# Float64 weights joined by one VectorE instruction, their signs taken over by GpSimd, and maxima and splits over pairs of chunks

## The chip, the core and the metric

The kernel runs on one core of a Trainium2 chip. The metric is the device time of one execution in microseconds (us). The engines are named as in the profile: PE is TensorE's matmul and PEld its weight load, DVE is VectorE, ACT is ScalarE, POOL is GpSimd, SP is SyncE, which here issues all DMAs.

## The reference

Causal attention with a window of 128 and an ALiBi bias over 8 batches of 8 heads, 576 positions and 64 features, then a feed-forward layer over the 4608 tokens that come out. The sizes are 512 to 2048 to 512.

```python
scores = scale * np.matmul(q, k.transpose(0, 1, 3, 2))
scores = np.where(mask, scores + bias[None], -1000000000.0)
attn = np.exp(scores - np.max(scores, axis=-1, keepdims=True))
attn = attn / (np.sum(attn, axis=-1, keepdims=True) + 1e-09)
x = np.matmul(attn, v)                       # then to (4608, 512)
h = x @ w_in                                 # w_in  (512, 2048)
g = 0.5 * h * (1.0 + erf(h * inv_sqrt2))
return g @ w_out                             # w_out (2048, 512)
```

The weights arrive as float64: `np.random.randn(...)` times a factor, with no cast. The kernel must therefore make float32 values of 64-bit words on the chip, before it can use them.

## The kernel before, in words

**Stages.** Batch 0 of the attention runs in float32 (`softmax_first`, `turn`, `weigh`). Tile 0 of the feed-forward layer (512 tokens) follows: `mlp_in(0, ...)` on PE at L600, then `mlp_out(0, ...)`, half of it in float32 against the float32 weights `zo` (L654), half of it in float16 against `wo` (L661). Batch 1 of the attention runs between these matmuls. From then on there is one batch and one tile per turn, up to tile 8. Float16 operands are pairs of halves, high and low, scaled by a power of two.

**The weights.** They come in 16 chunks of 128 partitions by 1024 values, each value a pair of 32-bit words (`raw`): eight chunks of `w_in` (names `zi`, then `wi`) and eight of `w_out` (names `zo`, then `wo`). SP fetches them at L176 and L179. Each chunk goes through `to_float32` (L182):

- ACT, L190: the high word read as a float32, its absolute value times 2^-112 into `z`.
- ACT, L192: the low word turned into the three bits that follow the high word's mantissa, written over the low word as int32.
- DVE, L195: `z` limited from above, with its maximum as a by-product (`accum_out=stat`).
- DVE, L196: `z` shifted left by 3, joined with the low bits.
- DVE, L199: the sign bit of the high word joined in.

**Scales.** The maximum of each pair of chunks goes over the partitions with `partition_all_reduce` on POOL (L114). From it DVE makes a power of two, `pww`, and its inverse, `sww`. With these, `split_weights` (L203) makes the high half on ACT (L207) and the low half on DVE (L149), for each chunk by itself. For `w_out` there is one such scale for all eight chunks together, `stwo` (L259), from which `pwm`, `k2` and `s2` follow (L260 to L270). Without them no float16 `wo` can be made, and without `pwm` no output tile can be scaled.

**Other users of POOL at that time.** The same all-reduce serves the maxima of v for batches 0 and 1 (`stv`) and of q and k for batch 1 (`stq`); the q and k halves of batch 1, and so its scores, wait for `stq`. Memsets clear `kbuf`'s pad (L377), the rooms of `e_main` (L448, L449) and, as soon as DVE has written them, the masked corners of the scores (L442). From tile 1 on, POOL also scales `g` (L627), and from batch 3 on `e_main` (L519).

**The order.** Each engine works through its own queue in order. Which order that is, a scheduler decides when the program is built. Where an instruction of POOL needs a routine that is not in the library that GpSimd holds, the built program has an instruction ahead of it that reloads the library. The order prints that as `ISA` with no tile behind it. Library 1 holds the all-reduce, library 0 holds `tensor_scalar`; memsets need neither. The program has three such reloads: of library 0 near the start (it is resident then), of library 1 ahead of the first all-reduce, and of library 0 ahead of the first L627.

Of the kernel before, what the change touches and what calls it, by code (L numbers as in the profile page):

```python
# [20 lines left out]
P = 128  # L21
# [37 lines left out]
def attention_gelu_mlp(  # L59
# [14 lines left out]
    def small(shape, name, bufs, tag=None, dt=F32):  # L74
        return pool.tile(shape, dt, tag=tag or name, name=name, bufs=bufs)
# [34 lines left out]
    def over_partitions(stat, n, early=False, floor=FLOOR):  # L110


        if early:
            nc.gpsimd.partition_all_reduce(stat, stat, P, bass_isa.ReduceOp.max)  # L114
            nc.vector.tensor_scalar_max(stat, stat, floor)
# [44 lines left out]
    hi_thr = 122848.0 * SQUEEZE  # L160
    STAT_FLOOR = 2.0 ** ((127 - 50) // 8 - 127) * (1 + (127 - 50) % 8 / 8)
    assert FLOOR == 2.0 ** -50
    NW = NCC * 256

    raws = {}
# [13 lines left out]
            nc.sync.dma_start(flat.rearrange("p (c f) -> p c f", c=2), w_out_v[:, 2 * m : 2 * m + 2, :])  # L179
        raws[n] = raw  # L180

    def to_float32(n, z, stat):  # L182
# [12 lines left out]
        nc.vector.tensor_scalar(z, z, hi_thr, None, op0=ALU.min, op1=ALU.max, accum_out=stat)  # L195
        nc.vector.scalar_tensor_tensor(  # L196
            out=zi, in0=zi, scalar=3, in1=lo, op0=ALU.logical_shift_left, op1=ALU.bitwise_or
        )
        nc.vector.scalar_tensor_tensor(  # L199
            out=zi, in0=hi, scalar=-0x80000000, in1=zi, op0=ALU.bitwise_and, op1=ALU.bitwise_or  # L200
        )

    def split_weights(z, both, scale):  # L203

        hi = both[:, 0].rearrange("p c f -> p (c f)")
        lo = both[:, 1].rearrange("p c f -> p (c f)")
        nc.scalar.activation(hi, z, AF.Copy, scale=scale)  # L207
        low_part(lo, z, scale, hi)

    def pow2_of_words(dst, stat):  # L210

        nc.vector.tensor_scalar(
            dst.bitcast(I32), stat.bitcast(I32), 3, EXPMASK, op0=ALU.logical_shift_left, op1=ALU.bitwise_and
        )

    def absmax(dst, src, axis=AX.X):
        nc.vector.tensor_reduce(out=dst, in_=src, axis=axis, op=ALU.max, apply_absolute_value=True)  # L217
# [4 lines left out]
    pwo = pool.tile([P, NWP], F32, name="pwo")  # L222
    stwo = pool.tile([P, NWP], F32, name="stwo")

    def weights_in(ns, gate=None):

        zs = {}
        stat = small([P, len(ns)], f"stw{ns[0]}", 1)
        for n in ns:
            if n % 2 == 0:  # L230
                tag, bufs = Z_TAGS[n // 2]
                zz = pool.tile([P, 2, NW], F32, tag=tag, name=f"zi{n}", bufs=bufs)
            zs[n] = zz[:, n % 2]
            if gate is not None:
                nc.vector.tensor_copy(zs[n][:, 0:1], gate)
            to_float32(n, zs[n], stat[:, n - ns[0] : n - ns[0] + 1])
        over_partitions(stat, len(ns), True, STAT_FLOOR)
        r = slice(ns[0], ns[-1] + 1)

        nc.vector.tensor_tensor(out=stat[:, 0:1], in0=stat[:, 0:1], in1=stat[:, 1:2], op=ALU.max)  # L240
        pow2_of_words(pww[:, r], stat[:, 0:1].broadcast_to([P, len(ns)]))
        inverse(sww[:, r], pww[:, r], 12)
        tile_scales(0, ns)
        for n in ns:
            both = pool.tile([P, 2, NCC, 256], F16, name=f"wi{n}")
            split_weights(zs[n], both, sww[:, n : n + 1])
            wi.append(both)

    def weights_out_raw(m):

        if m % 2 == 0:
            zo.append(pool.tile([P, 2, NW], F32, tag="wo", name=f"zo{m}", bufs=4))
            zo.append(zo[m])
        to_float32(NWP + m, zo[m][:, m % 2], stwo[:, m : m + 1])

    def weights_out_scale():


        over_partitions(stwo, NWP, True, STAT_FLOOR)  # L259
        pow2_of_words(pwo, stwo)  # L260
        nc.vector.tensor_tensor(out=pwo, in0=pwo, in1=pww, op=ALU.mult)
# [13 lines left out]
    def weights_out_split(m):  # L275

        tag, bufs = ("wo", 4) if m else ("ld", 2)
        both = pool.tile([P, 2, 2, 2, DM], F16, tag=tag, name=f"wo{m}", bufs=bufs)
        for k in range(2):
            split_weights(zo[m + k][:, k], both[:, k], s2[:, m + k : m + k + 1])  # L280
            wo[m + k] = both[:, k]
        held.append(both)
        if m + 2 == NWP:
            first = pool.tile([P, 2, 2, 2, DM], F16, tag="wo", name="wo_first", bufs=4)
            nc.sync.dma_start(first, held[0])
            wo[0], wo[1] = first[:, 0], first[:, 1]
# [940 lines left out]
```

## Time and profile before

| what | us |
|---|---|
| median of 3 runs (lowest, highest) | 940.12 (938.73, 943.64) |
| span of the profiled execution, first to last instruction | 936.4 |
| busy in it: PE, DVE, ACT, POOL | 900.2, 737.2, 555.9, 199.0 |
| first `mlp_in` matmul on PE | 72.97 |
| all-reduce of `stq`, of `stwo` (start) | 106.07, 115.91 |

The span is 3.7 us below the median, for what lies around the first and the last instruction. In a timeline a row gives start, length, engine, line, operation, tiles and, in brackets, the engine's idle time ahead of it with what ended that. In a row by line or tile, the numbers behind the bar are busy us in total and the mean length of one in ns; three numbers with slashes are the least, the median and the greatest length in ns.

### The profile page before, as it was taken

Reading aid. Unit: us, or ns where it says so; the run is one execution under the profiler, and the core shown is the slowest. Engines: PE = TensorE matmul, PEld = TensorE weight load, DVE = VectorE, ACT = ScalarE, POOL = GpSimd, SP = SyncE. Lnnn points to the kernel's source line nnn. Section 1 sums busy time; section 2 is a strip of 40 time slices with the busy share of each in tenths; the row PEclk is TensorE's granted clock in tenths of the full one; section 3 lists DMA queues with packets and bytes.
Section 4 is the critical chain, followed back from the end, with each engine's and each line's share of the span. In section 5 each row is a group of like instructions: output and inputs, shape, how many; then the busy total and the mean of one; then the engine's idle time right before and its main releaser. Section 6 shows DMA issues by size and latency. Waiting matters only on the chain.

```text
span 936.4 us, 18792 instructions
## 1 busy us (share of the span) xinstructions
PE 900.2 (96%) x7500; PEld 487.0 (52%) x7500; DVE 737.2 (79%) x1445; ACT 555.9 (59%) x1175; POOL 199.0 (21%) x412
## 2 busy tenths in 40 slices
PE   7969999779999899999999999999999999999998
PEld 3544444434454445444454445444444444488887
DVE  6898989779876877678767877687646898999771
ACT  5977958777673566256435643575465545744760
POOL 1010000013201443135303531164114540000000
PEclk9989999999999999999999999999999999999999
DMA  9518433872456133614562446224402351001001
GB/s 319 215 46 298 173 107 74 199 203 57 86 137 157 36 66 78 197 36 76 97 164 69 62 102 176 69 51 83 104 13 51 71 84 46 1 12 35 1 1 46
DMA packets 173512, 91.26 MB, mean 97 GB/s; under 512 B 132592, under 2 KB 155248, under 8 KB 173296
## 3 DMA queue, kind: packets, MB, share of 16 engines
q1 hardware_dynamic: 173424, 90.06, 38.6%
q8 instruction: 59, 0.97, 0.4%
q14 instruction: 29, 0.24, 0.1%
HBM read 46.53 MB, written 9.44 MB: 60 GB/s over the span
## 4 chain that ended last, share of the span: by engine, by line
PE 53%; DVE 19%; ACT 8%; DMA 4%; issue 3%; SPq 1%; POOL 0%; POOLq 0%; DVEq 0%; ACTq 0%
PE o L661 22%; PE h L600 17%; PE av L559 3%; PE sc L415 3%; DMA v<-vp 2%; ACT s L510 2%; PE u L860 2%; PE u_out L947 2%; DVE g L149 2%; DVE e_main L149 2%; DVE nmax L507 1%; PE v L860 1%; DMA et<-e_main 1%; DVE stv L217 1%; DVE s L437 1%
## 5 line engine op out<-in xcount | busy, mean ns | idle before, releaser
L600 PE MATMUL h<-x,wi 128*128 128x512 f16 x1536 | 341.1, 380 | 6.1 <-ACT g L626 3.1
L600 PEld LDWEIGHTS <-wi 128*128 128x128 f16 x1536 | 147.5, 98 | 184.7 <-issue 9.0
L661 PE MATMUL o<-wo,g 128*128 128x512 f16 x936 | 213.0, 380 | 1.1 <-DVE wo L149 1.1
L661 PEld LDWEIGHTS <-g 128*128 128x128 f16 x1248 | 117.2, 98 | 141.5 <-issue 2.3
L510 ACT ACTIVATE s<-s,nmax 128x192 f32<-128x192 f32 x252 | 111.2, 442 | 96.9 <-DVE nmax L507 93.3
L627 POOL TENSOR_SCALAR g<-g,sg 128x512 f16<-128x512 f32 x96 | 77.9, 817 | 192.0 <-ACT g L626 189.8
L149 DVE SCALAR_TENSOR_TENSOR e_main<-s,z,e_main 128x192 f16<-128x192 f32 x252 | 107.0, 468 | 13.1 <-POOL e_main L519 8.9
L519 POOL TENSOR_SCALAR e_main<-s,z 128x192 f16<-128x192 f32 x180 | 93.0, 534 | 86.9 <-issue 31.3
L626 ACT ACTIVATE g<-h,gs 128x512 f32<-128x512 f32 x96 | 63.9, 687 | 74.5 <-PE h L600 51.8
L149 DVE SCALAR_TENSOR_TENSOR g<-g,sg,g 128x512 f16<-128x512 f32 (+1 forms) x112 | 90.3, 824 | 21.0 <-POOL g L627 19.4
L415 PE MATMUL sc<-kbuf,qbuf 64*64 64x192 f16 (+1 forms) x1656 | 74.8, 263 | 9.2 <-DMA kbuf<-kp 4.5
L437 DVE SCALAR_TENSOR_TENSOR s<-sc,cs,bias_h 128x384 f32<-128x384 f32 x112 | 63.8, 608 | 12.2 <-PE sc L415 12.0
L661 PE MATMUL o<-wo_first,g 128*128 128x512 f16 x312 | 71.8, 379 | 0.1
L507 DVE TENSOR_REDUCE nmax<-s 128x5 f32<-128x960 f32 (+1 forms) x56 | 58.6, 1046 | 2.2 <-POOL s L442 0.2
L442 POOL MEMSET s<- 64x128 f32 (+1 forms) x112 | 19.1, 171 | 186.7 <-DVE s L437 186.1
L572 ACT ACTIVATE x<-av,cx 128x448 f16<-128x448 f32 (+6 forms) x52 | 23.5, 474 | 58.0 <-PE av L559 57.9
L415 PEld LDWEIGHTS <-qbuf 64*64 64x64 f16 x1512 | 36.0, 106 | 38.4 <-issue 36.9
L559 PE MATMUL av<-et,vbuf 128*64 128x128 f16 (+1 forms) x1680 | 44.1, 211 | 6.4 <-DMA et<-e_main 6.3
L559 PEld LDWEIGHTS <-vbuf 128*64 128x64 f16 x1680 | 41.0, 111 | 16.6 <-issue 11.3
L510 ACT ACTIVATION_READ_ACCUMULATOR s<-s,nmax 128x1 f32 x252 | 47.1, 187 | 0.0
L510 ACT ACT_TABLE_LOAD x29 | 37.2, 1283 | 7.9 <-DVE square L120 7.4
L947 PEld LDWEIGHTS <-g 128*128 128x128 f16 x384 | 37.6, 98 | 4.6
(268 smaller groups left out, 1159.7 us busy)
## 6 DMA issues: line engine op xcount, KB each, us to landing
v<-vp SPq DMA_DIRECT2D x32, 320.0 KB, 5.5
out<-ob SPq DMA_DIRECT2D x34, 256.0 KB, 2.3
raw<-w_in SPq DMA_DIRECT2D x8, 1024.0 KB, 13.7
raw<-w_out SPq DMA_DIRECT2D x8, 1024.0 KB, 5.1
q<-qp SPq DMA_DIRECT2D x7, 1152.0 KB, 6.2
k<-kp SPq DMA_DIRECT2D x7, 1152.0 KB, 6.3
qbuf<-qp SPq DMA_DIRECT2D x4, 288.0 KB, 4.9
kbuf<-kp SPq DMA_DIRECT2D x4, 288.0 KB, 5.2
```

Of the source, the lines that this page charges most:

```text
L149: nc.vector.scalar_tensor_tensor(out=dst, in0=src, scalar=scale, in1=high, op0=ALU.mult, op1=ALU.subtract)
L415: nc.tensor.matmul(ps[bank][o, n, 0:W], a, m, start=(i == 0), stop=(i == len(terms) - 1 and b > 0), skip_group_check=True,)
L437: nc.vector.scalar_tensor_tensor(out=s[:, bank[0] : bank[0] + k, :], in0=ps[bank][:, 0:k, 0:W], scalar=cs, in1=bias.broadcast_to([P, k, W] ...
L507: nc.vector.tensor_reduce(out=nmax[:, r], in_=s[:, r], axis=AX.X, op=ALU.max, negate=True)
L510: nc.scalar.activation(s[:, i, :], s[:, i, :], AF.Exp, bias=nmax[:, i : i + 1], accum_out=z[:, i : i + 1])
L519: nc.gpsimd.tensor_scalar(e[:, i, 0, c], s[:, i], z[:, i : i + 1], 1.0, op0=ALU.mult, op1=ALU.mult)
L559: nc.tensor.matmul(av[r, (j - blocks[0]) * QB : (j - blocks[0] + len(js)) * QB], v32s[b][:, hp, kb, r] if b < EXACT else vbuf[:, vi, hp, k ...
L600: nc.tensor.matmul(ph, wi[n][:, a, cc, k * P : (k + 1) * P], x[:, cc, b, :], start=(i == 0), stop=(i == 3 * NCC - 1),)
L626: nc.scalar.activation(g32, ph, AF.Gelu, scale=gsc[t, n])
L627: nc.gpsimd.tensor_scalar(g[:, r, 0], g32, gsg[t, n], 1.0, op0=ALU.mult, op1=ALU.mult)
L661: nc.tensor.matmul(o, both[:, a, c], wo[n][:, b, k, :], start=(fc == first and i == 0), stop=(fc == last and i == 2),)
L947: nc.tensor.matmul(ps[name][:, tb], f(d, a)[:, k, tb * P : (tb + 1) * P], w(d, b, k), start=first, stop=True, skip_group_check=True,)
```

## The change

**Each chunk.** The limit from above (L195) goes, and with it the maximum as a by-product. The sign is made in place on POOL: the upper 16 bits of the high word, read as int16, become -32768 or 0 (`tensor_scalar` with `is_lt` and `mult`, one per chunk, on 1024 values that stand 8 bytes apart). ACT writes the low bits as int16 into the lower 16 bits of the same high word. So the high word now holds sign and low bits, and one DVE instruction (L197 in the new file) shifts `z` and joins that word in. It waits for ACT and for POOL.

**Each pair of chunks.** A maximum over 2048 values replaces the two by-products (`absmax`, L211), one all-reduce has one column in place of two, and one ACT and one DVE instruction over 2048 values split the pair (L203, L150). For `w_out`, `stwo` has four columns in place of eight.

```diff
         zi = z.bitcast(I32)
+        quarters = raw.rearrange("p f w -> p (f w)").bitcast(I16).rearrange("p (f q) -> p f q", q=4)
+        low_bits, sign = quarters[:, :, 2], quarters[:, :, 3]
         nc.scalar.activation(z, hi.bitcast(F32), AF.Abs, scale=SQUEEZE)
+        nc.gpsimd.tensor_scalar(sign, sign, 0.0, -32768.0, op0=ALU.is_lt, op1=ALU.mult)
         nc.scalar.activation(
-            lo, lo.bitcast(U32), AF.Copy, bias=-0.5 + 7.5 * 2.0 ** -18, scale=2.0 ** -29 * (1 - 2.0 ** -18)
-        )
-        nc.vector.tensor_scalar(z, z, hi_thr, None, op0=ALU.min, op1=ALU.max, accum_out=stat)
-        nc.vector.scalar_tensor_tensor(
-            out=zi, in0=zi, scalar=3, in1=lo, op0=ALU.logical_shift_left, op1=ALU.bitwise_or
+            low_bits, lo.bitcast(U32), AF.Copy, bias=-0.5 + 7.5 * 2.0 ** -18, scale=2.0 ** -29 * (1 - 2.0 ** -18)
         )
         nc.vector.scalar_tensor_tensor(
-            out=zi, in0=hi, scalar=-0x80000000, in1=zi, op0=ALU.bitwise_and, op1=ALU.bitwise_or
+            out=zi, in0=zi, scalar=3, in1=hi, op0=ALU.logical_shift_left, op1=ALU.bitwise_or
         )
...
-            to_float32(n, zs[n], stat[:, n - ns[0] : n - ns[0] + 1])
-        over_partitions(stat, len(ns), True, STAT_FLOOR)
+            to_float32(2 * n + k, z[:, k])
+        z = z.rearrange("p k f -> p (k f)")
+        absmax(stat, z)
+        over_partitions(stat, 1, True)
...
-        for n in ns:
-            both = pool.tile([P, 2, NCC, 256], F16, name=f"wi{n}")
-            split_weights(zs[n], both, sww[:, n : n + 1])
+        both = pool.tile([P, 2, 2, NCC, 256], F16, name=f"wi{n}")
+        hi, lo = (both[:, a].rearrange("p k c f -> p (k c f)") for a in range(2))
+        split_weights(z, hi, lo, sww[:, 2 * n : 2 * n + 1])
...
-        to_float32(NWP + m, zo[m][:, m % 2], stwo[:, m : m + 1])
+        to_float32(NWP + m, zo[m][:, m % 2])
+        if m % 2:
+            absmax(stwo[:, m // 2 : m // 2 + 1], zo[m].rearrange("p k f -> p (k f)"))
```

**The order on POOL.** Before, from the first all-reduce (`stv` of batch 0) to that of `stwo`. L114 is the all-reduce, `stw` the maxima of a pair of `w_in` chunks, L377, L448 and L449 are memsets:

```order
L114 ISA
L114 ISA stv_307<-stv_307 128x1 [waits DVE_49]
L114 ISA stw_659<-stw_659 128x2 [waits DVE_49]
L377 MEMSET kbuf 128x2x128 [waits DMAHW1_49,DMAHW4_49,PE_49,Pool_49]
L114 ISA stw_686<-stw_686 128x2 [waits DVE_49]
L448 MEMSET e_main 128x10x64 [waits PE_49,Pool_49]
L114 ISA stw_715<-stw_715 128x2 [waits DVE_49]
L449 MEMSET e_main 128x8x64 [waits PE_49,Pool_49]
L114 ISA stw_744<-stw_744 128x2 [waits DVE_49]
L114 ISA stq_1141<-stq_1141 128x2 [waits DVE_49,Activation_49]
L114 ISA stv_1126<-stv_1126 128x1 [waits DVE_49]
L114 ISA stwo<-stwo 128x8 [waits DVE_49]
```

One reload stands ahead of the first all-reduce, and none follows among these. Now, on POOL, from the first all-reduce to that of the second pair (L115 is the all-reduce, L193 the sign, L373 and L444 memsets):

```order
L115 ISA stv_307<-stv_307 128x1 [waits DVE_49]
L193 ISA
L193 TENSOR_SCALAR raw_119<-raw_119 128x1024 [waits DMAHW6_49,Activation_49]
L193 TENSOR_SCALAR raw_121<-raw_121 128x1024 [waits DMAHW7_49,Activation_49]
L373 MEMSET kbuf 128x2x128 [waits DMAHW1_49,DMAHW4_49,PE_49,Pool_49]
L193 TENSOR_SCALAR raw_123<-raw_123 128x1024 [waits DMAHW0_49,Activation_49]
L193 TENSOR_SCALAR raw_125<-raw_125 128x1024 [waits DMAHW1_49,Activation_49]
L115 ISA
L115 ISA stw_659<-stw_659 128x1 [waits DVE_49]
L193 ISA
L193 TENSOR_SCALAR raw_127<-raw_127 128x1024 [waits DMAHW2_49,Activation_49]
L193 TENSOR_SCALAR raw_129<-raw_129 128x1024 [waits DMAHW3_49,Activation_49]
```

Signs and all-reduces alternate, and at each turn a reload stands between them. Between the all-reduce of `stv` and that of `stq` (batch 1) there are now 12 reloads, 13 signs, 5 all-reduces and the 3 memsets; in the whole program there are 17 reloads in place of 3. The place on POOL where `stq` and `stwo` stand (L438 are the memsets on the scores of batch 1):

```order
L115 ISA stq_1117<-stq_1117 128x2 [waits Activation_49]
L193 ISA
L193 TENSOR_SCALAR raw_977<-raw_977 128x1024 [waits DMAHW1_49,DVE_49,Activation_49]
L193 TENSOR_SCALAR raw_934<-raw_934 128x1024 [waits DMAHW2_49,DVE_49,Activation_49]
L193 TENSOR_SCALAR raw_1019<-raw_1019 128x1024 [waits DMAHW3_49,DVE_49,Activation_49]
L438 MEMSET s_0_1156 64x128 [waits DVE_49] x2
L438 MEMSET s_0_1156 64x64 [waits DVE_49]
L115 ISA
L115 ISA stwo<-stwo 128x4 [waits DVE_49]
```

The all-reduce of `stwo` has moved behind three memsets on the scores of batch 1, which themselves exist only after `stq`; before, it stood ahead of all of them.

More of the change, by code (lines that the diff above doesn't have):

```diff
@@ L13 @@
 I32 = mybir.dt.int32
+I16 = mybir.dt.int16
 U32 = mybir.dt.uint32
@@ L159, in attention_gelu_mlp @@
     SQUEEZE = 2.0 ** -112
[L160 to L162 removed]
+    NPW = NWP // 2
     NW = NCC * 256
@@ L221, in attention_gelu_mlp, with weights_in @@
     sww = pool.tile([P, NWP], F32, name="sww")
[L222 to L228, printed above, removed]
[L229 to L247 removed]
+    pwo = pool.tile([P, NPW], F32, name="pwo")
+    stwo = pool.tile([P, NPW], F32, name="stwo")
+    def weights_in(n, gate=None):
+        stat = small([P, 1], f"stw{n}", 1)
+        tag, bufs = Z_TAGS[n]
+        z = pool.tile([P, 2, NW], F32, tag=tag, name=f"zi{n}", bufs=bufs)
+        for k in range(2):
+            if gate is not None:
+                nc.vector.tensor_copy(z[:, k, 0:1], gate)
+            to_float32(2 * n + k, z[:, k])
+        z = z.rearrange("p k f -> p (k f)")
+        absmax(stat, z)
+        over_partitions(stat, 1, True)
+        r = slice(2 * n, 2 * n + 2)
+        pow2_of_words(pww[:, r], stat.broadcast_to([P, 2]))
+        inverse(sww[:, r], pww[:, r], 12)
+        tile_scales(0, [2 * n, 2 * n + 1])
+        both = pool.tile([P, 2, 2, NCC, 256], F16, name=f"wi{n}")
+        hi, lo = (both[:, a].rearrange("p k c f -> p (k c f)") for a in range(2))
+        split_weights(z, hi, lo, sww[:, 2 * n : 2 * n + 1])
+        wi.extend(both[:, :, k] for k in range(2))
     def weights_out_raw(m):
@@ L253, in weights_out_raw @@
             zo.append(zo[m])
[L254 removed]
+        to_float32(NWP + m, zo[m][:, m % 2])
+        if m % 2:
+            absmax(stwo[:, m // 2 : m // 2 + 1], zo[m].rearrange("p k f -> p (k f)"))
     def weights_out_scale():
[L259 removed]
+        over_partitions(stwo, NPW, True)
         pow2_of_words(pwo, stwo)
[L261 removed]
+        nc.vector.tensor_tensor(out=pwo, in0=pwo, in1=pww[:, 0:NWP:2], op=ALU.mult)
         most = pool.tile([P, 1], F32, name="most")
@@ L278, in weights_out_split @@
         both = pool.tile([P, 2, 2, 2, DM], F16, tag=tag, name=f"wo{m}", bufs=bufs)
+        hi, lo = (both[:, a].rearrange("p k c f -> p (k c f)") for a in range(2))
+        split_weights(zo[m].rearrange("p k f -> p (k f)"), hi, lo, s2[:, m : m + 1])
         for k in range(2):
-            split_weights(zo[m + k][:, k], both[:, k], s2[:, m + k : m + k + 1])
-            wo[m + k] = both[:, k]
+            wo[m + k] = both[:, :, k]
         held.append(both)
@@ L1067, in attention_gelu_mlp @@
     gates = [None, (1, 'z', 8), (2, 'z', 8), (3, 'z', 8)]
-    for n in range(0, NWP, 2):
-        g = gates[n // 2]
-        weights_in([n, n + 1], g and getattr(unit(0, g[0]), g[1])[:, g[2] : g[2] + 1])
+    for n in range(NPW):
+        g = gates[n]
+        weights_in(n, g and getattr(unit(0, g[0]), g[1])[:, g[2] : g[2] + 1])
     fetch(2)
```

12 lines of the change are left out of this document (4 added, 8 removed).

## The prediction, before the result was known

> **What bounds the kernel now.** The page comes first: it tells the busy shares and the chain of work that ended last.
>
> ```profile
> span 936.4 us, 18792 instructions
> PE 900.2 (96%) x7500; PEld 487.0 (52%) x7500; DVE 737.2 (79%) x1445; ACT 555.9 (59%) x1175; POOL 199.0 (21%) x412
> PE 53%; DVE 19%; ACT 8%; DMA 4%; issue 3%; SPq 1%; POOL 0%; POOLq 0%; DVEq 0%; ACTq 0%
> ```
>
> PE is busy for 96% of the span, and POOL has no share in the chain. But the change touches only the stage in which the weights are made ready, so the busy times by windows of 25 us come next (PE, PEld, DVE, ACT, POOL; then granted clock, DMA share, GB/s).
>
> ```profile
> 0.00:25.00 25.00, 19.25 (x137) 9.58 (x137) 16.13 (x41) 15.31 (x40) 2.57 (x14) 1.00 0.97 323
> 25.00:50.00 25.00, 22.91 (x199) 14.13 (x197) 20.70 (x59) 24.57 (x68) 2.20 (x3) 0.93 0.48 177
> 50.00:75.00 25.00, 17.19 (x124) 11.84 (x125) 24.54 (x51) 15.68 (x26) 3.40 (x5) 0.80 0.29 95
> 75.00:100.00 25.00, 25.00 (x118) 11.29 (x117) 22.54 (x36) 23.58 (x39) 0.00 (x0) 1.00 0.76 263
> 100.00:125.00 25.00, 25.00 (x95) 11.37 (x94) 24.96 (x40) 24.35 (x33) 2.16 (x3) 1.00 0.33 126
> ```
>
> Here DVE and ACT are the busy engines beside PE, and POOL works 10.33 us in 125 (the sum of its column). PE has idle time only before 75 us: 5.75, 2.09 and 7.81 us, 15.65 in all. A DVE that is relieved can win no more than that; POOL has much room, if its work doesn't have to stand in a row with what others wait for. So the last view is POOL's timeline of the stage (start, length, and in brackets the idle time ahead).
>
> ```profile
> 1.59 0.29 POOL masks.py:199 TENSOR_SCALAR_AFFINE_SELECT adders<-adders 128x128 bf16<-128x128 bf16 x1 [0.29 <-POOL kbuf L301]
> ...
> 19.37 0.38 POOL L114 PARTITION_ALL_REDUCE stv<-stv  x1 [16.36 <-DVE z L478]
> 26.11 1.26 POOL L114 PARTITION_ALL_REDUCE stw<-stw  x1 [6.36 <-DMA raw<-w_in]
> 30.30 0.31 POOL L377 MEMSET kbuf<- 128x256 f16 x1 [2.92 <-PE sc L415]
> 49.38 1.26 POOL L114 PARTITION_ALL_REDUCE stw<-stw  x1 [18.77 <-DVE zi L195]
> 52.99 0.63 POOL L448 MEMSET e_main<- 128x640 f16 x1 [2.35 <-PE tp L496]
> 56.55 0.35 POOL L114 PARTITION_ALL_REDUCE stw<-stw  x1 [2.92 <-DVE pww L212]
> 56.77 0.59 POOL L449 MEMSET e_main<- 128x512 f16 x1
> 66.82 1.32 POOL L114 PARTITION_ALL_REDUCE stw<-stw  x1 [9.45 <-DVE zi L195]
> 106.07 0.35 POOL L114 PARTITION_ALL_REDUCE stq<-stq  x1 [37.94 <-ACT kbuf L363]
> 108.00 0.37 POOL L114 PARTITION_ALL_REDUCE stv<-stv  x1 [1.57 <-DVE stq L115]
> 115.91 1.44 POOL L114 PARTITION_ALL_REDUCE stwo<-stwo  x1 [7.54 <-DVE zo L195]
> ...
> 132.15 0.14 POOL L442 MEMSET s<- 64x64 f32 x1 [0.71 <-DVE s L437]
> ```
>
> Between 19.75 (19.37 + 0.38) and 106.07 POOL has 86.32 us for five all-reduces and three memsets; that is the room into which 12 reloads and 13 signs are now put.
>
> **What DVE, ACT and PE win.** By line and form, up to 190 us (busy us, mean ns):
>
> ```profile
> L149 DVE SCALAR_TENSOR_TENSOR wi<-zi,sww,wi 128x1024 f16<-128x1024 f32 x8 | 10.1, 1280 | 0.0
> ...
> L199 DVE SCALAR_TENSOR_TENSOR zi<-raw,zi 128x1024 int32<-128x1024 int32 x8 | 9.8, 1223 | 0.0
> L196 DVE SCALAR_TENSOR_TENSOR zi<-zi,raw 128x1024 int32<-128x1024 int32 x8 | 9.7, 1227 | 0.0
> ...
> L195 DVE TENSOR_SCALAR_CACHE_REDUCE zi<-zi 128x1024 f32<-128x1024 f32 x8 | 9.7, 1213 | 0.0
> ...
> L217 DVE TENSOR_REDUCE stv<-v 128x1 f32<-128x2560 f32 x3 | 8.5, 2817 | 3.4 <-DMA v<-vp 3.4
> ...
> L149 DVE SCALAR_TENSOR_TENSOR vbuf<-v,scv,vbuf 128x2560 f16<-128x2560 f32 x1 | 2.9, 2886 | 0.0
> ```
>
> And ACT's high halves in the same view:
>
> ```profile
> L207 ACT ACTIVATE wi<-zi,sww 128x1024 f16<-128x1024 f32 x8 | 8.8, 1151 | 2.0 <-DVE sww L144 2.0
> ...
> L372 ACT ACTIVATE kbuf<-k,scq 128x2304 f16<-128x2304 f32 x1 | 2.3, 2304 | 0.0
> ```
>
> - Conversion, 16 chunks: three instructions (1.21 + 1.23 + 1.22 = 3.66) become one join (1.23) and half of a maximum over 2048 (2817 ns / 2560 = 1.10 ns per value, 2.25 for the pair, 1.13 per chunk). That saves 1.30 each, 21 us of DVE.
> - Low halves, 8 pairs: two of 1.28 become one of 2048 at 2886 / 2560 ns each, 2.31. That saves 0.25 each, 2 us. ACT saves as much on the high halves (two of 1.15 become one of 2.05 at 1.00 ns per value); its low-bits writes stay 16 in number, and that 16-bit writes cost it the same is an assumption. No DMA is added or taken away.
>
> Most of these 23 us lie beside PE's full windows after 75 us and are worth nothing there. They would count ahead of 75 us, and only where no wait takes their place.
>
> **What POOL gets: the sign.** No row shows a compare, an int16 operand or a stride of 8 bytes on POOL. The nearest are its other `tensor_scalar` lines (least, median, greatest ns):
>
> ```profile
> L627 POOL TENSOR_SCALAR g<-g,sg x96: 684/772/1819, 204.8 to 735.1; 128x512 f16<-128x512 f32 x96
> L519 POOL TENSOR_SCALAR e_main<-s,z x180: 418/425/1819, 316.5 to 770.6; 128x192 f16<-128x192 f32 x180
> ```
>
> From the fastest of both, (684 - 418) / 320 = 0.83 ns per value: 0.42 + 832 × 0.83 = 1.11 us for 1024 values. By the slowest L627, 1819 / 512 = 3.55 ns per value: 3.64 us. I take the slow end, since all three of those features are strange to the fast rows, and a stride gains nothing. It could be beyond: twice is 7.3.
>
> **What POOL gets: the reload.** An idle row bounds it from below: the affine select at 1.59 came 0.29 us after the memset, with a reload of the library that was already there. From above there are the 16.36 us ahead of the first all-reduce, which DVE ended and not the reload, so it is no more than that. What a reload does is to read code from DRAM; the nearest rows are the reads of the raw weights in the same stretch (issue to landing):
>
> ```profile
> DMA to landing us min/median/max: 5.0/7.5/14.7
> ```
>
> I take the median, 7.5 us, with all of 0.3 to 16.4 kept as bounds. I assume that none of it runs ahead: the signs behind it and the all-reduce before it stand in one queue, and code in use can't be overwritten.
>
> The GPSIMD Engine Reference of the Trainium skill (§ 2.1, Instruction dispatch) has about 6 us for the first call to a freshly loaded kernel, with no instruction to be seen. By that price in place of 7.5 the sum below would be 977 us of span, about 981; no run shown here bears on it.
>
> **The sum.** Call a reload p and a sign s. The order puts all of this in one row on POOL, and in it nothing can pass. The all-reduce of `stq` then starts no sooner than
>
> 19.75 + 12p + 13s + 4.56 (the five all-reduces: 1.26, 1.26, 0.35, 1.32, 0.37) + 1.53 (memsets: 0.31, 0.63, 0.59) = 25.84 + 12p + 13s.
>
> With 7.5 and 3.64 that is 163.2, where it was 106.07. This takes it that POOL never waits in this row for a raw chunk. SP fetches those in order, each as soon as a join has freed its room, and before, they ran ahead of the chain:
>
> ```profile
> 62.28 0.37 SPq L179 DMA_DIRECT2D raw<-w_out  x1
> ...
> 90.94 0.37 SPq L352 DMA_DIRECT2D k<-kp  x1
> ```
>
> Five chunks of `w_out` have their signs in this row, and k of batch 1, from which `stq` is made, is fetched behind them in SP's queue. If POOL were once caught waiting for such a fetch, from the join that frees the room, it would cost one landing, 7.5 us by the row above, and so more for k; I count none, since POOL has two signs and two reloads of other chunks to do meanwhile, and leave it to the range. Behind `stq` comes what followed it before: the halves of batch 1, its scores, and their memsets, up to 132.15 + 0.14, so 26.2 us. In the new order one more reload stands behind those (p), then the all-reduce of `stwo`; three signs lie in the 26.2 beside the halves and the scores. The steps behind `stwo` on DVE, of which seven remain, take 0.13 to 0.18 each if nothing is in between, about 1.0 in all:
>
> ```profile
> 118.38 0.17 DVE L115 TENSOR_SCALAR stwo<-stwo 128x8 f32<-128x8 f32 x1
> ...
> 139.32 0.14 DVE L144 TENSOR_SCALAR k<-pwm 128x1 int32<-128x1 int32 x1
> ```
>
> So `k` stands at 25.84 + 12p + 13s + 26.2 + p + 1.44 + 1.0. Before, it stood at 139.32, and 936.4 - 139.32 = 797.1 us came behind it: the float16 `wo` (L661 can't start without), all further tiles and batches, PE full. I keep that remainder. The end is then 851.6 + 13 (p + s), and with 11.14 for p + s 996.4, which is 60 us more. The profiled execution's span is 3.7 us below the median of the runs, so the time is about 1000 us. The change gives even when p + s = (936.4 - 851.6) / 13 = 6.5.
>
> DVE's 23 us don't come off: while POOL is the bound, DVE waits at the joins (L197), and in its queue the softmax of batch 0 and the maxima stand behind them; PE, whose `mlp_in` needs the `wi` pairs, idles with it.
>
> **The rivals.**
> - *The shared lock.* POOL's signs may be held up by DVE. The Trainium skill's page SBUF — State Buffer (Who interferes with whom) says that the port pair that DVE and POOL share is an exclusive lock, held for a whole instruction. The trace does not bear that out for POOL:
>
> ```profile
> 434.34 2.32 POOL L519 TENSOR_SCALAR e_main<-s,z 128x192 f16<-128x192 f32 x5 [3.95 <-ACT s L510]
> ...
> 434.80 1.56 DVE L149 SCALAR_TENSOR_TENSOR e_main<-s,z,e_main 128x192 f16<-128x192 f32 x3 [0.61 <-POOL e_main L519]
> ```
>
>   Five of POOL took 0.46 each, against 0.418 at the fastest, while DVE ran two-input instructions. If each of the 13 signs waited out one such of 1.2 us, the end would be 16 later, 1016.
> - *A dear sign or reload.* p + s over 14.6 gives over 1041 of span: twice the sign with the same reload (14.8) does it. 1045 and more.
> - *Hidden reloads, no change.* If p is near 0.3, as in the idle row, with s at 3.64, `stq` is free at 77 and stays at 106.07, where ACT's L363 ended the wait; what is won by DVE ahead of 75 us and what `stwo` loses about cancel: 940. For it speaks that rooms for two libraries might exist; against it that the program then needs no reload.
> - *Faster.* If POOL's row ends by 95, so 12p + 13s up to 69, neither `wi` nor `stq` waits for POOL, DVE's relief fills PE's idle time: 15.65 less what goes by before the first load is there (row below), 11 us, 925.3 of span, 929. It decides at p + s near 5.5; the fast sign (1.11) needs a reload under 4.5, below the fastest read in the row above.
>
> ```profile
> 4.54 2.20 PE L415 MATMUL sc<-kbuf,qbuf 64*64 64x192 f32 x20 [4.54 <-DMA kbuf<-kp]
> ```
>
> **How the numbers follow.** About 0.5%, 4.7 us, is what a measurement can tell here. Forecast (p + s from 7 to 14.6): 0.74. Lock: 0.08. Dear: 0.05. Both of these are slower too, 0.87 together. No change: 0.08. Faster: 0.05. The range: low by a fast sign and the cheapest read with a little on top (p + s = 7.3, 946 of span, 950); high by twice the sign (1041 and 3.7, 1045). It leaves out nearly all of the last two cases and half of the dear one.
>
> **What would show it.** In the new profile: idle times of 5 us and more on POOL ahead of each change between all-reduce and sign (p), the length of L193 (s), `stq` near 163, `stwo` some 34 us behind it, and about 797 us from `k` to the end; PE idle in windows after 75 us that were full. Wrong: `stq` still near 106, idle times under 3 us, or a rest behind `k` that shrinks because PE catches up.

## The result, and the profile after

The changed kernel takes 1020.1 us (median of 4 runs, 1014.7 to 1021.0), the kernel before 939.5 (4 runs, 938.7 to 943.6): a ratio of 1.084, with a 95% interval of 1.081 to 1.086. The profiled execution has a span of 1017.9 us, 81.5 more than before. The page of the changed kernel, with the chain's shares by engine last:

```profile
span 1017.9 us, 18799 instructions
PE 921.5 (91%) x7500; PEld 493.8 (49%) x7500; DVE 731.4 (72%) x1393; ACT 574.5 (56%) x1167; POOL 279.2 (27%) x428
PE 48%; DVE 21%; ACT 13%; issue 7%; DMA 6%; POOL 4%; SPq 1%; POOLq 0%; DVEq 0%; ACTq 0%
```

DVE has lost only 5.8 us of work, ACT has gained 18.6, POOL 80.2. POOL has 4% of the chain, and "issue", which had 3%, has 7%. A part of the reloads is among that: the profile has no busy row for a reload and, where nothing else ended the wait, names it "issue". The windows of 25 us (same columns as before) show where the time went:

```profile
75.00:100.00 25.00, 14.91 (x83) 6.90 (x83) 6.54 (x13) 22.50 (x25) 8.31 (x6) 0.81 0.33 96
100.00:125.00 25.00, 13.34 (x50) 5.14 (x50) 9.57 (x13) 7.04 (x13) 9.81 (x3) 0.77 0.15 47
125.00:150.00 25.00, 15.03 (x52) 5.82 (x53) 15.59 (x18) 17.01 (x19) 9.72 (x4) 0.70 0.41 137
150.00:175.00 25.00, 21.26 (x63) 9.02 (x62) 7.60 (x14) 13.05 (x17) 11.54 (x4) 0.84 0.32 121
```

In the 50 us from 75 to 125, PE was busy throughout before and is busy for 28.25 us now; DVE went from 47.50 to 16.11, ACT from 47.93 to 29.54. Over the whole span PE's idle time grew by 60.2 us (from 36.2 to 96.4). Its busy time grew by 21.3 for the same 7500 matmuls; the clock granted in these four windows is 0.70 to 0.84, where it was 1.00 from 75 us on before. POOL, busy for 8 to 12 us in each window, looks idle for more than half of the time as well, and that is the trap of a busy share. Its timeline tells what it does in between:

```profile
19.24 0.38 POOL L115 PARTITION_ALL_REDUCE stv<-stv  x1 [16.23 <-DVE z L474]
29.75 10.14 POOL L193 TENSOR_SCALAR raw<-raw 128x1024 int16<-128x1024 int16 x2 [10.13 <-PE sc L423]
39.70 0.40 POOL L373 MEMSET kbuf<- 128x256 f16 x1
43.02 10.18 POOL L193 TENSOR_SCALAR raw<-raw 128x1024 int16<-128x1024 int16 x2 [2.92 <-ACT zi L191]
58.93 0.38 POOL L115 PARTITION_ALL_REDUCE stw<-stw  x1 [5.73 <-DVE z L474]
66.35 10.19 POOL L193 TENSOR_SCALAR raw<-raw 128x1024 int16<-128x1024 int16 x2 [7.04 <-PE tp L492]
...
82.85 0.38 POOL L115 PARTITION_ALL_REDUCE stw<-stw  x1 [5.78 <-issue]
...
94.60 10.07 POOL L193 TENSOR_SCALAR raw<-raw 128x1024 int16<-128x1024 int16 x2 [10.91 <-issue]
112.47 0.38 POOL L115 PARTITION_ALL_REDUCE stw<-stw  x1 [7.79 <-issue]
120.24 10.07 POOL L193 TENSOR_SCALAR raw<-raw 128x1024 int16<-128x1024 int16 x2 [7.40 <-ACT g L613]
138.46 0.38 POOL L115 PARTITION_ALL_REDUCE stw<-stw  x1 [8.15 <-issue]
145.97 11.49 POOL L193 TENSOR_SCALAR raw<-raw 128x1024 int16<-128x1024 int16 x2 [7.13 <-ACT raw L194]
163.46 0.38 POOL L115 PARTITION_ALL_REDUCE stv<-stv  x1 [6.00 <-issue]
171.30 5.16 POOL L193 TENSOR_SCALAR raw<-raw 128x1024 int16<-128x1024 int16 x1 [7.46 <-issue]
182.23 0.37 POOL L115 PARTITION_ALL_REDUCE stq<-stq  x1 [5.77 <-issue]
189.58 17.38 POOL L193 TENSOR_SCALAR raw<-raw 128x1024 int16<-128x1024 int16 x3 [6.98 <-issue]
...
219.47 0.39 POOL L115 PARTITION_ALL_REDUCE stwo<-stwo  x1 [5.92 <-issue]
```

The reader is to see a gap of 5.7 us or more at each change between all-reduce and sign, whatever releaser is named, and signs of 5 us. Between 19.62 and 182.23 the twelve gaps are 89.3 us (10.13, 5.73, 7.04, 5.78, 10.91, 7.79, 7.40, 8.15, 7.13, 6.00, 7.46, 5.77), 7.4 each, and the 13 signs about 67. The steps on the raw chunks and on `k` (least, median, greatest ns in the first two):

```profile
L194 ACT ACTIVATE raw<-raw x16: 2458/2488/2590, 20.6 to 192.2; 128x1024 int16<-128x1024 uint32 x16
L193 POOL TENSOR_SCALAR raw<-raw x16: 5075/5145/7482, 29.7 to 199.5; 128x1024 int16<-128x1024 int16 x16
```

```profile
221.76 0.14 DVE L145 TENSOR_SCALAR k<-pwm 128x1 int32<-128x1 int32 x1
```

From `k` to the end there are 796.1 us, against 797.1 before: everything was lost ahead of it.

### The profile page after: what moved, and what is told of

It reads as the page before. It is cut to its first block, busy times and chain, and to the rows that moved or that the text cites. A ratio compares the mean times of both kernels' runs of the same rounds, so it can differ in the third digit from the quotient of the medians.

```text
span 1017.9 us, 18799 instructions
## 1 busy us (share of the span) xinstructions
PE 921.5 (91%) x7500; PEld 493.8 (49%) x7500; DVE 731.4 (72%) x1393; ACT 574.5 (56%) x1167; POOL 279.2 (27%) x428
## 4 chain that ended last, share of the span: by engine, by line
PE 48%; DVE 21%; ACT 13%; issue 7%; DMA 6%; POOL 4%; SPq 1%; POOLq 0%; DVEq 0%; ACTq 0%
PE o L657 21%; PE h L596 14%; PE sc L411 3%; POOL raw L193 3%; PE av L555 3%; DMA v<-vp 2%; ACT raw L194 2%; ACT s L506 2%; PE u L856 2%; DVE g L150 2%; PE u_out L943 2%; DVE e_main L150 1%; DVE stv L211 1%; DVE nmax L503 1%; PE v L856 1%
## 5 line engine op out<-in xcount | busy, mean ns | idle before, releaser
L596 PE MATMUL h<-x,wi 128*128 128x512 f16 x1536 | 351.6, 387 | 35.7 <-DVE wi L150 15.3
L657 PE MATMUL o<-wo,g 128*128 128x512 f16 x936 | 215.8, 383 | 5.3 <-ACT wo L203 4.3
L657 PEld LDWEIGHTS <-g 128*128 128x128 f16 x1248 | 118.0, 98 | 147.0 <-issue 8.9
L150 DVE SCALAR_TENSOR_TENSOR e_main<-s,z,e_main 128x192 f16<-128x192 f32 x252 | 107.7, 470 | 13.2 <-POOL e_main L515 7.9
L515 POOL TENSOR_SCALAR e_main<-s,z 128x192 f16<-128x192 f32 x180 | 92.4, 531 | 86.9 <-issue 31.3
L411 PE MATMUL sc<-kbuf,qbuf 64*64 64x192 f16 (+1 forms) x1656 | 78.0, 268 | 32.1 <-DVE qbuf L150 11.1
L150 DVE SCALAR_TENSOR_TENSOR g<-g,sg,g 128x512 f16<-128x512 f32 (+1 forms) x112 | 90.0, 823 | 19.5 <-POOL g L623 19.4
L193 POOL TENSOR_SCALAR raw<-raw 128x1024 int16<-128x1024 int16 x16 | 84.7, 5374 | 60.0 <-issue 25.3
L438 POOL MEMSET s<- 64x128 f32 (+1 forms) x112 | 19.1, 171 | 172.0 <-DVE s L433 166.1
L503 DVE TENSOR_REDUCE nmax<-s 128x5 f32<-128x960 f32 (+1 forms) x56 | 58.5, 1045 | 2.1 <-POOL s L438 0.2
```

The source lines that it names most:

```text
L150: nc.vector.scalar_tensor_tensor(out=dst, in0=src, scalar=scale, in1=high, op0=ALU.mult, op1=ALU.subtract)
L193: nc.gpsimd.tensor_scalar(sign, sign, 0.0, -32768.0, op0=ALU.is_lt, op1=ALU.mult)
L411: nc.tensor.matmul(ps[bank][o, n, 0:W], a, m, start=(i == 0), stop=(i == len(terms) - 1 and b > 0), skip_group_check=True,)
L503: nc.vector.tensor_reduce(out=nmax[:, r], in_=s[:, r], axis=AX.X, op=ALU.max, negate=True)
L515: nc.gpsimd.tensor_scalar(e[:, i, 0, c], s[:, i], z[:, i : i + 1], 1.0, op0=ALU.mult, op1=ALU.mult)
L596: nc.tensor.matmul(ph, wi[n][:, a, cc, k * P : (k + 1) * P], x[:, cc, b, :], start=(i == 0), stop=(i == 3 * NCC - 1),)
```

## The experiments

Theory A is the prediction's: reloads and signs add up in POOL's one queue, and the stage ends when that row does. Rivals: ACT's low bits (B), now 2.49 us a chunk where they took 1.17; the one late maximum per pair (C); the signs by themselves or the reloads by themselves. Each kernel's order is made anew by the scheduler, so an edit can also move other instructions. Each ratio is to the kernel before on the same chip: 938.4 us for the first three, 938.8 for 5 to 8, 938.4 for 9 to 12.

**1. Sign on VectorE.** The changed kernel with

```diff
-        nc.gpsimd.tensor_scalar(sign, sign, 0.0, -32768.0, op0=ALU.is_lt, op1=ALU.mult)
+        nc.vector.tensor_scalar(sign, sign, 0.0, -32768.0, op0=ALU.is_lt, op1=ALU.mult)
```

> The changed kernel with one edit: the sign instruction is issued on VectorE in place of GpSimd, same operands. Three reloads are left, as in the kernel before. Theory A (reloads and signs add up in POOL's one queue and nothing else matters): the 80 us go; stq is no longer held by POOL and stands near 106, the end is at 930 to 955. Rival B (ACT's low bits, 2.49 us a chunk in the changed kernel against 1.17 before, 21 us in all, are what costs most of it): stays above 970. Rival C (one maximum per pair comes too late and holds the mlp_in matmuls): stays above 970 too, with PE waiting for wi while POOL has no work.

959.2 us, ratio 1.022 (1.020 to 1.024): some 60 of the 81 us go with POOL's signs and the reloads. By A `stq` should stand near 106 and the end be at most 955:

```profile
115.52 0.37 POOL L115 PARTITION_ALL_REDUCE stq<-stq  x1 [33.10 <-ACT kbuf L359]
```

It stands at 115.5 and waits for ACT, not for POOL. The time lies between A's 955 and the 970 above which B or C was to be the larger cause. So A explains the larger part, and some 20 us have another cause.

**2. Signs on POOL, maxima on VectorE.** No library is reloaded:

```diff
-        over_partitions(stat, 1, True)
+        over_partitions(stat, 1)
...
-        over_partitions(stwo, NPW, True)
+        over_partitions(stwo, NPW)
...
-        pwv[b], scv[b] = pow2(f"v{b}", stat, 1, 3, b < 2)
+        pwv[b], scv[b] = pow2(f"v{b}", stat, 1, 3)
...
-        pw, sc = pow2(f"q{b}", stat, 2, 2, b < 2)
+        pw, sc = pow2(f"q{b}", stat, 2, 2)
```

> The changed kernel with the signs left on POOL, but all early maxima over the partitions made by VectorE (the path that later batches use), so that no library is ever reloaded after the start. Theory A: POOL's queue holds 16 signs of 5.15 us, 82 us from about 20 us on, with nobody else's work behind them but memsets; the last sign ends near 105 to 125, and the time is 935 to 965. If the signs alone are the cost (rival D: a sign of 5.15 us holds DVE's joins, reloads or not): above 985.

963.9 us, 1.026 (1.023 to 1.029), near the upper end of what A has: with 16 signs of 5.17 us (median) on POOL it takes 5 us more than experiment 1. The two kernels differ by more than these signs: here VectorE makes the maxima, there it makes the 16 signs, 1.32 us each.

**3. Short signs, reloads kept.**

```diff
+        nc.gpsimd.tensor_scalar(sign[:, 0:64], sign[:, 0:64], 0.0, -32768.0, op0=ALU.is_lt, op1=ALU.mult)
```

> The changed kernel with the sign made on 64 of a chunk's 1024 values only; the other values keep mantissa bits where low bits and sign should stand, so this part of the computation is left out. The reloads stay (the program has 8 between the all-reduces of stv and stq, where the changed kernel has 12). Theory A with the reload at 7.4 us each: POOL's row to stq is 19.6 + 8 x 7.4 + 13 x 0.35 + 3 = 86, so stq is hardly held, and the time is 930 to 955. If the reloads are the cost by themselves (they hold what others wait for, wherever they stand): above 970.

964.4 us, 1.029 (1.025 to 1.032), between the two expectations. With the reloads that are left, 8 ahead of `stq`, it takes 5 us more than experiment 1. Measured from that kernel, which is no clean zero since VectorE makes the signs in it, signs alone add 5, reloads alone add 5, and both in one queue some 60: each fits beside the others' work, the sum doesn't. `stq` came at 133.8, not 86, and it waited for ACT: the row gives the end only where the row is full.

**4. The prices alone.** A kernel of its own, nothing else on the core.

> A kernel of its own that computes nothing of the reference (zeros go out). On POOL alone, 1024 values per partition: the sign as it is (int16, 8 bytes apart, compare); the same without a compare (times, plus); int16 without gaps; float32 without gaps with compare; float32 8 bytes apart; float32 to float16 with two factors (the form of the g scaling). Then four all-reduces and tiny tensor_scalar in turn (reloads with no other work on the core), ACT's low bits as int16 8 bytes apart, as int32 8 bytes apart and as int16 without gaps, and DVE's two-input instruction on float32 alone and beside three signs. If the stride costs, both strided forms are near 5 us and int16 without gaps near 1.1; if int16 costs, int16 without gaps is near 5 us and strided float32 near 1.1; if the compare costs, only the compares are slow. Reload by the changed kernel's rows: 5.8 to 7.5 us. If DVE and POOL lock each other out, signs beside DVE are longer than alone, or DVE's 1.2 us are.

Its rows on POOL (L55 the sign as it is, L57 without a compare, L59 int16 without gaps, L61 float32 without gaps, L64 float32 8 bytes apart, L66 two factors to float16; L68, L72, L73 the reloads):

```profile
7.21 5.10 POOL L55 TENSOR_SCALAR raw_s<-raw_s 128x1024 int16<-128x1024 int16 x1
12.14 2.45 POOL L57 TENSOR_SCALAR raw_s4b<-raw_s4b 128x1024 int16<-128x1024 int16 x1
...
28.81 3.63 POOL L59 TENSOR_SCALAR c<-c 128x1024 int16<-128x1024 int16 x1
32.41 3.63 POOL L61 TENSOR_SCALAR f_out<-a 128x1024 f32<-128x1024 f32 x1
...
46.78 3.72 POOL L64 TENSOR_SCALAR f_out<-f_out 128x1024 f32<-128x1024 f32 x1
50.46 1.05 POOL L66 TENSOR_SCALAR h_out<-a 128x1024 f16<-128x1024 f32 x1
...
66.67 0.38 POOL L72 PARTITION_ALL_REDUCE stat<-stat  x1 [5.52 <-issue]
73.99 0.19 POOL L73 TENSOR_SCALAR tiny<-stat 128x1 f32<-128x1 f32 x1 [6.94 <-issue]
80.29 0.38 POOL L72 PARTITION_ALL_REDUCE stat<-stat  x1 [6.11 <-issue]
88.24 0.19 POOL L73 TENSOR_SCALAR tiny<-stat 128x1 f32<-128x1 f32 x1 [7.58 <-issue]
...
137.41 17.63 POOL L97 TENSOR_SCALAR raw_both<-raw_both 128x1024 int16<-128x1024 int16 x3
```

The compare costs most: 5.10 against 2.45 on the same 16-bit values 8 bytes apart, and 3.63 without gaps in either type, where two factors (to float16) take 1.05. On top, 16-bit values 8 bytes apart cost 1.5 (5.10 against 3.63), float32 8 bytes apart nearly nothing. A reload is 5.5 to 6.1 us ahead of an all-reduce and 6.9 to 7.6 ahead of `tensor_scalar`. ACT, alone as well (L79 low bits as int16 8 bytes apart, L82 as int32, L85 int16 without gaps, three of them):

```profile
119.08 2.44 ACT L79 ACTIVATE raw_act<-raw_act 128x1024 int16<-128x1024 uint32 x1
121.27 1.15 ACT L82 ACTIVATE raw_act<-raw_act 128x1024 int32<-128x1024 uint32 x1
...
125.69 3.38 ACT L85 ACTIVATE c16b<-raw_act 128x1024 int16<-128x1024 uint32 x3
```

Only the 16-bit write with gaps is dear. And DVE's two-input instruction alone (L92) and beside three signs (L99):

```profile
129.53 7.52 DVE L92 SCALAR_TENSOR_TENSOR d<-d,d 128x1024 f32<-128x1024 f32 x6
...
137.27 22.39 DVE L99 SCALAR_TENSOR_TENSOR d<-d,d 128x1024 f32<-128x1024 f32 x16
```

1.25 us alone, 1.40 on average beside POOL; the signs 5.88 in place of 5.1. They hinder each other a little. Had each waited out the other's whole instructions, the 16 and the 3 together would have taken 16 × 1.25 + 3 × 5.1 = 35.3 us, and it was 22.4.

**5. Sign on VectorE, low bits as int32.** Experiment 1 with

```diff
-            low_bits, lo.bitcast(U32), AF.Copy, bias=-0.5 + 7.5 * 2.0 ** -18, scale=2.0 ** -29 * (1 - 2.0 ** -18)
+            lo, lo.bitcast(U32), AF.Copy, bias=-0.5 + 7.5 * 2.0 ** -18, scale=2.0 ** -29 * (1 - 2.0 ** -18)
```

> The first experiment (sign on VectorE) with ACT writing the low bits as int32 over the low word again, as before the change; they are not joined in, so this part of the computation is left out. The first experiment was 20 us slower than the kernel before with POOL out of the way. Theory B' (of those 20 us the larger part is ACT's: 2.44 us for a 16-bit write 8 bytes apart against 1.15 for a 32-bit one, alone on the core, 21 us in 16 chunks): 937 to 947. Theory C (the pair's single maximum comes too late): stays at 953 to 962, with ACT's write at 1.17.

949.6 us, 1.012 (1.009 to 1.014). Between the expectations: about 10 of the 20 us are ACT's writes, about 10 are not.

**6. Pairs only.** The changed kernel with no sign on POOL, int32 low bits, and two joins:

```diff
+            lo, lo.bitcast(U32), AF.Copy, bias=-0.5 + 7.5 * 2.0 ** -18, scale=2.0 ** -29 * (1 - 2.0 ** -18)
...
+            out=zi, in0=zi, scalar=3, in1=lo, op0=ALU.logical_shift_left, op1=ALU.bitwise_or
...
+            out=zi, in0=hi, scalar=-0x80000000, in1=zi, op0=ALU.bitwise_and, op1=ALU.bitwise_or
```

> The changed kernel without the single join: low bits as int32 by ACT and two VectorE joins, as before the change; one maximum, one split and one scale per pair are kept. VectorE saves 0.17 us a chunk and 0.25 a pair, 4.7 us in all, most of it beside full PE windows. Theory B': 934 to 941. Theory C (pairs come too late): 950 to 960.

938.9 us, 0.9993 (0.9979 to 1.0008): no difference. C falls; the pairs, alone, cost nothing and bring nothing.

**7. The changed kernel with low bits as int32.** The edit of 5, with signs on POOL.

> The changed kernel with ACT writing the low bits as int32 over the low word; they are not joined in, so this part of the computation is left out. Signs and reloads on POOL stay. Theory A (POOL's row alone sets the end of the stage; ACT's longer write lies beside it): 1005 to 1021. If ACT's 21 us add to POOL's row: 990 to 1002.

1005.0 us, 1.071 (1.069 to 1.073), at the edge of A's expectation, 15 us less than the changed kernel. But the order on POOL is another one here: the first all-reduce of `stw` stands behind three signs, not four, the last signs ahead of `stq` go together, and the all-reduce of `stwo` stands ahead of the memsets again:

```profile
145.62 20.07 POOL L193 TENSOR_SCALAR raw<-raw 128x1024 int16<-128x1024 int16 x4 [6.69 <-issue]
...
173.63 0.44 POOL L115 PARTITION_ALL_REDUCE stq<-stq  x1
...
204.57 0.39 POOL L115 PARTITION_ALL_REDUCE stwo<-stwo  x1 [13.69 <-DVE stwo L211]
```

From `stv` to `stq` there are 10 reloads and 14 signs, where the changed kernel has 12 and 13. At 7.4 and 5.15 us that alone is 9.7 us sooner; `stq` came 8.6 sooner and `k`, at 209.2, 12.6. The gaps with a reload are 7.5 us on average, as long as before. So A's row accounts for most of the 15 us, and the run doesn't show that ACT's longer write costs anything in the changed kernel.

**8. A sign without a compare, maxima on VectorE.**

```diff
+        nc.gpsimd.tensor_scalar(quarters[:, :, 1], sign, 32768.0, 0.0, op0=ALU.mult, op1=ALU.min)
...
+            out=zi, in0=zi, scalar=3, in1=lo, op0=ALU.logical_shift_left, op1=ALU.bitwise_or
```

> A version meant to beat both: the maxima over partitions on VectorE (no reload), ACT's low bits as int32, and the sign made without a compare (times 32768, then minimum with 0, int16 that saturates), written into the upper half of the low word, so that the single join stays. By the measuring kernel a sign without a compare takes 2.45 us against 5.08. Theory: POOL has 16 x 2.45 = 39 us with nothing waited for, VectorE saves 1.30 x 16 + 2 = 23 us less 7 maxima of about 1.6 = 11; the stage is 0 to 11 us shorter: 928 to 940. If the minimum costs what the compare costs, the signs are 5.1 us and it is 940 to 950. If the wait for ACT and POOL in series ahead of each join counts: 945 to 960.

958.2 us, 1.021 (1.019 to 1.022). A miss: the minimum costs what the compare costs. For that alone 940 to 950 was expected; 958.2 lies in the range given for waits on ACT and POOL ahead of each join, and this run doesn't show those by themselves.

```profile
L196 POOL TENSOR_SCALAR raw<-raw x16: 5132/5178/5517, 20.8 to 129.7; 128x1024 int16<-128x1024 int16 x16
```

**9. The changed kernel with a sign of factors alone.** The upper 16 bits are read as bfloat16 and multiplied by 0:

```diff
+        nc.gpsimd.tensor_scalar(sign.bitcast(BF16), sign.bitcast(BF16), 0.0, 1.0, op0=ALU.mult, op1=ALU.mult)
```

> The changed kernel with the sign made without a compare: the upper 16 bits read as bfloat16, times 0, times 1, which leaves a zero with the sign bit. By the measuring kernel a factor and a sum on 16-bit values 8 bytes apart take 2.45 us on POOL, the compare 5.08. The program has 8 reloads between the all-reduces of stv and stq (12 in the changed kernel), because shorter signs go together. Theory A by the row: 19.6 + 8 x 7.0 + 13 x 2.45 + 4 = 112 for stq, about as late as in the first experiment (115.5) where POOL had none: 957 to 972. If reloads are what counts whatever the signs take: above 985.

984.9 us, 1.049 (1.046 to 1.052): 35 us off, but 13 above A's expectation and at the edge of the 985 above which the reloads were to count by themselves. The signs take 2.48 us (median); `stq` comes at 145.5, not 112. By the trace 15 signs stand ahead of it, not 13, which makes A's row 116; waits of POOL in which no reload stands are 27 us more. Some of POOL's signs there:

```profile
104.73 4.78 POOL L193 TENSOR_SCALAR raw<-raw 128x1024 bf16<-128x1024 bf16 x2 [9.55 <-DMA raw<-w_out]
115.29 2.49 POOL L193 TENSOR_SCALAR raw<-raw 128x1024 bf16<-128x1024 bf16 x1 [5.78 <-DVE g L150]
121.38 2.48 POOL L193 TENSOR_SCALAR raw<-raw 128x1024 bf16<-128x1024 bf16 x1 [3.60 <-ACT zo L191]
...
137.20 2.48 POOL L193 TENSOR_SCALAR raw<-raw 128x1024 bf16<-128x1024 bf16 x1 [4.68 <-ACT zo L191]
```

Only ahead of the first row stands a reload, and a wait for a chunk of `w_out` with it; ahead of the others POOL waits with no reload at all, mostly for ACT. A row that is shorter isn't full any more: in the stretch from 85 to 150 us the chain of work that ended last spends 15.8% in ACT's low bits and 13.8% in fetches of `w_out`.

**10. Each sign twice.**

```diff
         nc.gpsimd.tensor_scalar(sign, sign, 0.0, -32768.0, op0=ALU.is_lt, op1=ALU.mult)
+        nc.gpsimd.tensor_scalar(sign, sign, 0.0, -32768.0, op0=ALU.is_lt, op1=ALU.mult)
```

> The changed kernel with every sign instruction issued twice (the second changes nothing), so a dose of the suspected cost. The program has 10 reloads and 25 signs between the all-reduces of stv and stq. Theory A by the row: 19.6 + 10 x 7.0 + 25 x 5.15 + 4 = 222 for stq, 40 more to the scale of w_out and 797 behind it: 1045 to 1075. If something else than POOL's row sets the end of the stage: within 15 us of 1020.

1071.9 us, 1.141 (1.138 to 1.144), as A has it; the row's 222 for `stq` is met within 2 us:

```profile
219.80 0.37 POOL L115 PARTITION_ALL_REDUCE stq<-stq  x1 [5.79 <-issue]
...
278.76 0.39 POOL L115 PARTITION_ALL_REDUCE stwo<-stwo  x1 [6.00 <-DVE z L510]
```

The end isn't met by the same steps: `k` came at 290.3, 70 us behind `stq` and not 40, and the rest took 779 and not 797. In this order 12 memsets on the scores of batch 1 stand ahead of `stwo`, where the changed kernel has 3, so more of batch 1 was done by then. The two misses cancel in part.

**11. Signs of factors, maxima on VectorE.** Kernel 8 with the sign of 9.

> The eighth kernel (958 us: maxima on VectorE, low bits as int32, sign into the low word's upper half) with the sign without a compare, as bfloat16 times 0. In the eighth the sign with a minimum took 5.14 us, as much as the compare, and POOL's 16 signs were back to back from 20.8 to 61 us. At 2.45 us a sign they end before the joins need them: 940 to 950. If the maxima on VectorE (7 chains of 12 small instructions) are what costs: 951 to 960.

957.4 us, 1.019 (1.017 to 1.022). A miss: signs of 2.50 in place of 5.18 bring nothing here. (In 8 only the first eight signs stood back to back up to 61 us; the others lie between 80.6 and 134.8, most of them behind waits for ACT.) The maxima on VectorE are the cause named in the expectation for such a time; this kernel has no control that shows it.

**12. VectorE's sign beside the high word.** Kernel 5 with the sign written into the low word's upper half:

```diff
+        nc.vector.tensor_scalar(quarters[:, :, 1], sign, 0.0, -32768.0, op0=ALU.is_lt, op1=ALU.mult)
...
+            out=zi, in0=zi, scalar=3, in1=lo, op0=ALU.logical_shift_left, op1=ALU.bitwise_or
```

> The fifth kernel (949.6 us: sign on VectorE in place in the high word, low bits as int32) with the sign written into the upper half of the low word, behind the low bits, and joined from there. In the fifth the sign overwrites what ACT's absolute value still has to read, so it waits for that; here it waits only for the low bits, which run ahead as before the change. VectorE has one instruction of 1.32 and one of 1.22 us a chunk in both. If that wait is the rest of the cost: 937 to 944. If it is the order or the 16-bit instruction itself: 946 to 953.

946.9 us, 1.008 (1.006 to 1.010). Its interval overlaps that of kernel 5, so the wait for ACT's absolute value is not shown to be the rest. Why one join and a 16-bit sign on VectorE are 8 to 11 us slower than two joins of the same length (938.9) stays open; the scheduler's other order was not tried by itself. It isn't the scale of `w_out` that is late: `k` stands at 137.9 in 5 and at 128.6 in 12, 139.3 before the change, and 807.7 and 816.0 us come behind it. No version that beats the kernel before was found.

## Why the prediction was right

1000 us was forecast, between 950 and 1045, and slower at 0.87; measured were 1020. The steps, for the profiled execution:

- *The reload* (7.5): 7.4 on average over the twelve. That it fits is luck, by a row that measures something else: alone a reload is 5.9 ahead of an all-reduce and 7.1 ahead of a sign by experiment 4, 6.5 on average or 78 us for twelve, and the other 11 us of the gaps are waits, which the prediction put at nothing. The GPSIMD Engine Reference of the Trainium skill (§ 2.1, Instruction dispatch), cited in the prediction with about 6 us, is borne out by the 5.5 to 6.1 ahead of an all-reduce; the way back is dearer.
- *The sign* (3.64): 5.15, the term that was mis-sized. 13 of them took 67.3 us in place of 47.3. That they'd be slow was taken from type, stride and compare together. The compare and the 16-bit stride did it, not the type, and one row, the slowest `g` scaling, couldn't give that size.
- *`stq`* (163.2): 182.2. The 19.0 more are 20.0 for the signs, 2.9 for a wait ahead of a sign that has no reload (40.10 to 43.02, behind ACT's Abs), less 2.7 for the five all-reduces (1.9 in place of 4.56), less 0.7 for the reloads; overlaps of rows make up the rest.
- *`stq` to `k`* (36.1 with the reload at 7.5): 39.5, of which 31.3 up to the last memset ahead of `stwo` in place of 26.2, 5.9 for the reload in place of 7.5, and 2.3 behind it in place of 2.4. *`k` to the end* (797.1): 796.1. 19.0 + 3.4 - 1.0 = 21.4, and from 996.4 to 1017.9 it is 21.5. The remainder behind `k` is no constant of the kernel: it is 797.4 in 7, but 779 in 10, 802.0 in 1 and 816.0 in 12. *From span to time* (3.7): 2.2.
- *ACT's 16-bit write* (an assumption, nothing): wrong, 1.3 us a chunk, 21 us of ACT, worth 10 us between experiments 1 and 5. What it costs in the changed kernel isn't shown: the chain of work that ended last passes these writes for 21 us in its first 230, but what run 7, without them, gains is for the most part that of its order.
- *DVE's 23 us* (worth nothing): worth nothing, but they weren't 23 either. DVE's busy time fell by 5.8. (PE also had 9.57 us of idle time between 175 and 200 before the change, beyond the 15.65 that the prediction counted; it made no difference here.) The joins grew by 4.5 in all (up to 240 us, by line; mean in ns), and so did other instructions:

```profile
L197 DVE SCALAR_TENSOR_TENSOR zo<-zo,raw 128x1024 int32<-128x1024 int32 x8 | 12.1, 1508 | 32.1 <-POOL raw L193 32.1
L197 DVE SCALAR_TENSOR_TENSOR zi<-zi,raw 128x1024 int32<-128x1024 int32 x8 | 12.1, 1506 | 25.2 <-POOL raw L193 25.2
```

- *POOL never waits for a raw chunk*: nearly so. Of the 162.6 us from `stv` to `stq` some 14 are waits, the 11 in the gaps and the 2.9 with no reload, and the chain that ended last passes fetches of `w_out` for 12 us in its first 230. With shorter signs (9) it mattered more.
- *The lock*: not as priced. The 16 signs were busy for 84.7 us by the page, 5.29 each, 0.2 more than alone, and not 1.2. But DVE waited for POOL at places, which the rival had the other way round. POOL's two signs from 29.75 end at 39.89; on DVE, in the changed kernel:

```profile
34.96 1.98 DVE L197 SCALAR_TENSOR_TENSOR zi<-zi,raw 128x1024 int32<-128x1024 int32 x1 [5.21 <-POOL raw L193]
...
37.59 2.54 DVE L474 TENSOR_SCALAR z<-z 128x4 f32<-128x4 f32 x1
44.93 1.21 DVE L197 SCALAR_TENSOR_TENSOR zi<-zi,raw 128x1024 int32<-128x1024 int32 x1
...
48.39 0.80 DVE L474 TENSOR_SCALAR z<-z 128x4 f32<-128x4 f32 x1
```

An instruction on four values, 0.17 us at the median of its line, lasts 2.54 and ends 0.24 behind the sign. The page SBUF — State Buffer of the Trainium skill (Who interferes with whom) has such an exclusive lock for DVE's one-input instructions in a two-port mode as well as for two-input ones; the first agrees with this row but not with the one at 48.39, which was done while the signs of 43.02 to 53.20 went on, and no row tells which mode either ran in. The second doesn't agree with the joins: the one at 44.93 ran beside the same signs with nothing added, and the six that began as the second sign of a pair or of three began took 1.97 to 2.01, 0.8 more and not a whole sign.

The mechanism was right where the row is nearly full (the changed kernel, experiments 7 and 10). It doesn't hold for shorter rows: A's ranges are missed by 13 us in 9, by 9 in 3 and by 4 in 1. Of the 20 us that are left in 1, ACT's write is about 10; the other 10 stay open.

## What to carry to other kernels

Before work is moved to an engine that looks idle, put what it will run in its queue's order, with what stands between: two kinds of instruction that need different libraries cost a reload of 6 to 7 us at each change, with no busy row, and the busy share of that engine won't show it. Price an instruction by operation, type and stride together, in a small kernel of its own: here the compare, and 16-bit values 8 bytes apart, each took the engine far from the rows that were at hand. And take the costs together, not one by one: over the kernel with the signs on VectorE, signs or reloads alone were 5 us, both some 60.

## What the runs showed of the hardware

- GpSimd's `tensor_scalar` on 1024 values: 1.05 us with two factors to float16, 3.63 with a compare; on 16-bit values 8 bytes apart 2.45 without and 5.1 with a compare, or with a minimum.
- ScalarE writes 16-bit values 8 bytes apart in 2.44 us per 1024, without gaps in 1.13 (3.38 / 3), and 32-bit ones 8 bytes apart in 1.15.
- The all-reduce takes 0.37 to 0.39 us for one, two or four columns in the changed kernel. Before, the same instruction on two columns has rows of 0.35 and of 1.26, so the longer ones are no matter of the columns.
